# Attention feeding a mixture of experts: w1's first load in eight pieces, one transfer each for a unit's q and k, and a changed first microsecond

## The chip, the cores and the metric

The kernel runs on one core of a Trainium2 chip. The metric is the device time in microseconds of one execution. A core has five engines with a program each: TensorE (PE in the profile, its weight loads PEld), VectorE (DVE), ScalarE (ACT), GpSimd (POOL) and SyncE (SP). SyncE computes nothing: it issues DMA transfers, which 16 DMA engines carry out.

## The reference

First comes attention in chunks of 64 rows, for 8 batches, 8 heads, 576 rows and a head size of 64; then the heads of a row are put side by side (512 values), and each row goes through one expert of eight. Which expert is a matter of the rows before it: where the local gate is at least 0.5, the row keeps the expert of the row before.

```python
scores = scale * np.matmul(q_c, k_c.transpose(0, 1, 2, 4, 3))    # per chunk of 64 rows
attn = np.exp(scores - max);  attn = attn / (sum + 1e-09)
x = np.matmul(attn, v_c)                                          # heads side by side: [8, 576, 512]
e = argmax(x[b, s] @ w_gate) if s == 0 or local_gate[b, s] < 0.5 else prev_e
out[b, s] = p[e] * (np.maximum(x[b, s] @ w1[e], 0) @ w2[e])       # w1[e]: 512 x 1024, w2[e]: 1024 x 512
```

All arrays are f32. q, k and v are 9.4 MB each; one expert's w1 is 2 MB, and so is its w2.

## The kernel before, in words

The attention is cut into 18 units of 256 rows with all 8 heads (`place`, L134). Units 6 and 15 are made of four leftovers of 64 rows (`mixed_rows`, L141). A unit's q and k are loaded by `load_qk` (L144): two transfers of 256 KB for q and two for k. The first holds heads 0 to 3, the second heads 4 to 7; a partition takes 8 rows of one head, 2 KB, from each. All these loads are issued by SyncE, except unit 0's k, which ScalarE issues (L154). The mixed units take eight transfers of 128 KB (L149). v comes in two or four transfers of 256-byte rows (`load_v`, L159).

Then, per unit: copies put two heads side by side (`pair_heads`, L172, done by GpSimd but for unit 0; its copies carry line L190 or, on ScalarE, L188), TensorE transposes q and k (`qk_transposes`, L209, by `trans4`, L198), multiplies them into scores (`scores`, L226, matmuls at L233), VectorE takes the row maximum and subtracts it (L244, L247), ScalarE takes the exponential (L252), TensorE transposes the result (`p_transposes`, L264) and multiplies it with v (`values`, L273, L282), VectorE normalises and writes the rows of x (L294 to L296), and these are transposed, multiplied with the gate weights (`router`, L318) and stored to the scratch tensor `x_d` by SyncE (L346).

TensorE, ScalarE, VectorE and GpSimd run in an order written out by hand (`PAR`, L50): "start" for the first microseconds, "steady" for the periods i = 1 to 15, "drain" for the end of attention and the first expert tiles. A period works on several units at once: it loads q and k of unit i+5 and v of unit i+2, pairs heads of unit i+3, transposes q and k of unit i+2, takes the scores of unit i+1 and the values of unit i-1, and stores x of unit i-2. SyncE's queue follows the order in which the program issues: in a period q and k, then v, then x's store, then, in some periods, a piece of w1.

Expert 0's w1 is loaded within the attention stage (`load_w1`, L101) in four transfers of 128 rows of 4 KB, 512 KB each, at the ends of periods 4, 6, 8 and 10 (L880 and L881). In periods 8 to 15 `split` (L107) turns half a piece per period into a high part (ScalarE) and a low part (GpSimd).

PSUM, where TensorE writes, has three buffers for transposes (`ps_tr`, L120), used in turn. In "start" the order for TensorE is q's transposes of unit 0 (tokens t0a, t0b), k's (t0c, t0d), four of unit 1, then unit 0's scores (s0).

After attention the expert stage runs tiles of 128 gathered rows through w1 and w2 of their expert; the change does not touch it.

## Time and profile before

| what | us |
|---|---|
| median of 3 runs | 638.35 (638.34 to 639.34) |
| the profiled execution, whole | 638.56 |
| its span, first to last instruction | 636.8 |
| TensorE busy in the span | 608.1 (96%) |
| VectorE, ScalarE, GpSimd busy | 380.3, 255.8, 147.0 |

The profile is of one execution, and the span is what all its views divide up; 1.76 us of the execution lie around it. Busy time of TensorE is pipelined and its ends are modelled, so a busy TensorE is not one at its peak. In a row of the order of time, the first number is the start, the second the length, "x8" the instructions merged in the row, and the brackets give how long the engine was idle before it and what ended that. "issue" there means that nothing which the profile shows ended the wait.

### The profile page before, as it was taken

What the parts mean: (1) busy time and instruction counts of PE and PEld (TensorE: products, weight loads), DVE (VectorE), ACT (ScalarE), POOL (GpSimd) and SP (SyncE); (2) the same over time, 40 slices, a digit from 0 to 9 for tenths busy, and PEclk for the clock granted to TensorE, in tenths of its full rate; (3) what the DMA queues carried; (4) which work ended last, traced back from release to release, by engine and by line L of the source; (5) the groups of instructions that cost most, each with busy time, mean ns of one, the idle gap of its engine ahead of it and who ended that gap; (6) DMA issues with size and microseconds to landing.
All of it is one profiled execution on the core that took longest, in us unless ns stands there. A gap on an engine that the chain in (4) does not pass through costs nothing. (4 is left out here: it accounts for less than half of the span.)

```text
span 636.8 us, 17170 instructions
## 1 busy us (share of the span) xinstructions
PE 608.1 (96%) x5904; PEld 513.6 (81%) x5904; DVE 380.3 (60%) x990; ACT 255.8 (40%) x468; POOL 147.0 (23%) x219
## 2 busy tenths in 40 slices
PE   4899989889999999999999999999999999999995
PEld 4788777777779788789998996789888998788884
DVE  2677678887795667575434556763478533387231
ACT  4677667664421252532112443421465211343120
POOL 3353244550050302021021021031021221010201
PEclk9999999999999999999999999999999999999999
DMA  8999999998440245155021264452086511054111
GB/s 267 264 265 301 284 272 264 303 286 271 158 150 21 71 151 185 44 178 180 20 70 55 61 206 134 151 178 64 27 271 203 190 52 59 30 184 147 65 30 36
DMA packets 78355, 97.83 MB, mean 154 GB/s; under 512 B 42672, under 2 KB 46768, under 8 KB 78192
## 3 DMA queue, kind: packets, MB, share of 16 engines
q1 hardware_dynamic: 71744, 75.30, 37.9%
q0 software_dynamic: 6160, 19.99, 9.6%
q8 instruction: 84, 1.38, 0.9%
q14 instruction: 79, 0.65, 0.3%
q10 hardware_dynamic: 288, 0.52, 0.3%
HBM read 76.62 MB, written 19.69 MB: 151 GB/s over the span
## 5 line engine op out<-in xcount | busy, mean ns | idle before, releaser
L804 POOL DMA_INDIRECT out<-ysb,sidx x38 | 40.2, 1058 | 356.3 <-DVEq L1028 160.6
L743 PE MATMUL y<-w2h,hq 128*128 128x512 f32 x368 | 119.8, 395 | 1.3 <-DVE ysb L1078 1.0
L743 PEld LDWEIGHTS y<-w2h,hq 128*128 128x128 f32 x368 | 69.1, 188 | 16.9 <-issue 2.5
L743 PE MATMUL y<-w2l,hq 128*128 128x512 f32 x184 | 71.9, 391 | 0.0
L1050 PE MATMUL tr<-xp,w1h 128*128 128x256 f32 x528 | 67.0, 283 | 0.0
L1050 PEld LDWEIGHTS tr<-xp,w1h 128*128 128x128 f32 x528 | 65.5, 192 | 1.2 <-ACT w2h L1011 0.4
L743 PE MATMUL y<-w2h,hp 128*128 128x512 f32 x192 | 63.3, 397 | 0.3 <-ACT hp L690 0.3
L722 PE MATMUL h<-w1h,xp 128*128 128x512 f32 x208 | 60.5, 396 | 0.0
L1058 ACT ACTIVATE hq<-tr 128x256 fp32r<-128x256 f32 x51 | 18.9, 383 | 68.4 <-PE tr L1050 44.8
L1078 DVE TENSOR_SCALAR ysb<-y,ppr 128x512 f32<-128x512 f32 x33 | 24.8, 751 | 34.4 <-PE y L743 30.3
L722 PEld LDWEIGHTS h<-w1h,xp 128*128 128x128 f32 x208 | 38.1, 188 | 7.4
L694 POOL DMA_INDIRECT xg<-x_d,gidx x36 | 38.5, 1069 | 19.8 <-issue 14.5
L743 PEld LDWEIGHTS y<-w2h,hp 128*128 128x128 f32 x192 | 36.0, 188 | 8.1 <-ACT hp L690 0.5
L789 ACT ACTIVATE hsb<-h 128x512 f32<-128x512 f32 x26 | 14.1, 596 | 66.1 <-PE h L722 49.1
L1059 DVE SCALAR_TENSOR_TENSOR hq<-tr,hq 128x256 fp32r<-128x256 f32 x51 | 21.1, 423 | 32.3 <-ACT hq L1058 28.6
L743 PEld LDWEIGHTS y<-w2l,hq 128*128 128x128 f32 x184 | 34.6, 188 | 6.9 <-DVEq L1028 0.3
L743 PE MATMUL y<-w2l,hp 128*128 128x512 f32 x96 | 37.5, 390 | 0.0
L1018 DVE TENSOR_TENSOR w1l<-raw,w1h 128x1024 fp32r<-128x1024 f32 x28 | 32.4, 1221 | 8.3 <-ACT w1h L1011 4.9
L691 DVE TENSOR_TENSOR xp<-tr,xp 128x512 fp32r<-128x512 f32 x39 | 25.5, 686 | 18.6 <-ACT xp L690 15.8
L1050 PE MATMUL tr<-xp,w1l 128*128 128x256 f32 x264 | 35.3, 283 | 0.0
L1018 DVE TENSOR_TENSOR w2l<-raw,w2h 128x1024 fp32r<-128x1024 f32 x28 | 32.8, 1223 | 1.2 <-issue 1.2
L1050 PEld LDWEIGHTS tr<-xp,w1l 128*128 128x128 f32 x264 | 33.3, 192 | 0.0
(242 smaller groups left out, 1152.7 us busy)
## 6 DMA issues: line engine op xcount, KB each, us to landing
raw<-in_moe_w SPq DMA_DIRECT2D x72, 512.0 KB
x_d<-xs SPq DMA_DIRECT2D x16, 528.0 KB
v<-in_v SPq DMA_DIRECT2D x20, 256.0 KB
qt<-in_q SPq DMA_DIRECT2D x16, 256.0 KB
lenth<-in_q SPq DMA_DIRECT2D x16, 256.0 KB
lentl<-in_k SPq DMA_DIRECT2D x16, 256.0 KB
kt<-in_k SPq DMA_DIRECT2D x14, 256.0 KB
raw<-in_v SPq DMA_DIRECT2D x6, 256.0 KB
```

Of the source, the lines that this page charges most:

```text
L691: lambda: V.tensor_tensor(lo, box["ps"], hi.bitcast(F32), ALU.subtract)]
L694: nc.gpsimd.indirect_dma_start(out=dst, out_offset=None, in_=src, in_offset=bass.IndirectOffsetOnAxis(ap=gidx[t].bitcast(U32), axis=0))
L722: nc.tensor.matmul(hs[:, j], xs[a][:, c], W1[w][c][:, 512 * j:512 * j + 512], start=(c == 0 and n == 0), stop=(c == 3 and n == 2))
L743: nc.tensor.matmul(y, h_of(t, f // 4)[a][:, f % 4], W2[w][c][:, f % 2, :], start=(f == 0 and n == 0), stop=(f == 7 and n == 2))
L789: nc.scalar.activation(hsb[:, 512 * j:512 * j + 512], hs[:, j], AF.Relu)
L804: nc.gpsimd.indirect_dma_start(out=out, out_offset=bass.IndirectOffsetOnAxis(ap=sidx[t].bitcast(U32), axis=0), in_=ysb, in_offset=None, bo ...
L1018: V.tensor_tensor(lo[c], raw[c], hi[c].bitcast(F32), ALU.subtract)
L1050: nc.tensor.matmul(hb[:, 256 * n:256 * n + 256], W1[w][c][:, P * (f + n):P * (f + n) + P], XP[:, x, c].rearrange("p s t -> p (s t)"), star ...
L1058: nc.scalar.activation(hi, ps, AF.Relu)
L1059: V.scalar_tensor_tensor(lo, ps, 0.0, hi.bitcast(F32), ALU.max, ALU.subtract)
L1078: V.tensor_scalar(ysb, y, pr, None, ALU.mult)
```

## The change

Three things change. Expert 0's w1 comes in eight transfers of 256 KB (128 rows of 2 KB), one at the end of each of the periods 4 to 11. For the units 1 to 15 that are not mixed, q is one transfer of 512 KB and so is k; the heads in the two column halves are then 0, 2, 4, 6 and 1, 3, 5, 7 instead of 0 to 3 and 4 to 7, and `values` reads v and writes x accordingly. For unit 0 the first halves of q and k go by SyncE's queue and the second halves by ScalarE's, and TensorE gets five matmuls of the identity with itself, 256 columns each, as its first work; their result is not read.

```diff
+    def heads_by_two(i):
+        return 0 < i < NS - 2 and not mixed_rows(i)
+
     def load_qk(i):
...
+                if heads_by_two(i):
+                    nc.sync.dma_start(
+                        dst.rearrange("p (j n) -> p j n", j=2),
+                        src[b, :, s0:s0 + n, :].rearrange("h (p r) d -> p h (r d)", r=8))
+                    continue
                 for j in range(2):
-                    (nc.scalar if i == 0 and src is k else nc.sync).dma_start(
+                    (nc.scalar if i == 0 and j == 1 else nc.sync).dma_start(
                         dst[:, 8 * D * j:8 * D * j + 8 * D],
                         src[b, 4 * j:4 * j + 4, s0:s0 + n, :].rearrange("g (p r) d -> p g (r d)", r=8))
...
-    def values(pT, vt, xs, fine=False):
+    def values(pT, vt, xs, fine=False, by_two=False):
         box = {}
+        if by_two:
+            xv = xs[:, :, 0:C].rearrange("p c (h j d) -> p j c h d", j=2, d=D)
+        else:
+            xv = xs[:, :, 0:C].rearrange("p c (j h d) -> p j c h d", j=2, d=D)
...
-                        vt[cp][64 * cc:64 * cc + 64, 4 * j + h, 0:D + 1],
+                        vt[cp][64 * cc:64 * cc + 64, 2 * h + j if by_two else 4 * j + h, 0:D + 1],
...
-                    xs[:, :, 256 * j:256 * j + 256].rearrange("p c (h d) -> p c h d", d=D),
+                    xv[:, j],
...
-        return values(pTs.pop(i), vts.pop(i), xss[i], fine)
+        return values(pTs.pop(i), vts.pop(i), xss[i], fine, heads_by_two(i))
...
         nc.scalar.activation(warm, ident[:, 0:1], AF.Exp)
+        awake = ps_tr.tile([P, 4, P], F32, name="tr")
+        for _ in range(5):
+            nc.tensor.matmul(awake[:, 0:2], ident, ident.unsqueeze(1).to_broadcast([P, 2, P]), start=True, stop=True)
...
-        if i in (4, 6, 8, 10):
-            load_w1(0, i // 2 - 2)
+        if 4 <= i < 12:
+            c, col = divmod(i - 4, 2)
+            col = slice(512 * col, 512 * col + 512)
+            nc.sync.dma_start(raw1[c][:, col], w1[0, P * c:P * c + P, col])
```

## Rows read from the trace of the kernel before

**Rows 1.** The page, its first part: busy time and instructions of each engine.

```profile
PE 608.1 (96%) x5904; PEld 513.6 (81%) x5904; DVE 380.3 (60%) x990; ACT 255.8 (40%) x468; POOL 147.0 (23%) x219
```

**Rows 2.** Busy time by stretch: PE, PEld, DVE, ACT, POOL, clock, DMA share, GB/s.

```profile
0.00:24.00 24.00, 14.23 (x306) 12.74 (x310) 8.88 (x16) 12.01 (x21) 8.80 (x30) 1.00 0.91 271
24.00:140.00 116.00, 106.51 (x2531) 88.46 (x2523) 90.30 (x256) 81.47 (x142) 55.62 (x109) 1.00 0.96 277
140.00:636.80 496.80, 487.40 (x3082) 412.43 (x3082) 281.13 (x720) 162.30 (x307) 82.56 (x80) 1.00 0.36 119
```

**Rows 3.** TensorE's waits between 24 and 140 us: total, times, longest.

```profile
PE sc L233 <- issue: 3.4, 5, 1.4
PE o L282 <- issue: 2.0, 2, 1.3
...
PE lg L324 <- issue: 0.7, 1, 0.7
```

**Rows 4.** The start in order of time, all engines, 0 to 16 us.

```profile
1.43 0.28 POOL masks.py:199 TENSOR_SCALAR_AFFINE_SELECT ident<-ident 128x128 f32<-128x128 f32 x1
...
5.59 0.61 POOL L190 COPY kr<-kt 128x512 f32<-128x512 f32 x1 [3.87 <-DMA kt<-in_k]
...
6.18 0.62 ACT L188 COPY qr<-qt 128x512 f32<-128x512 f32 x1 [2.62 <-DMA qt<-in_q]
...
6.95 1.94 PE L198 MATMUL tr<-ident,qr 128*128 128x128 f32 x8 [6.95 <-ACT qr L188]
...
8.68 1.92 PE L198 MATMUL tr<-ident,kr 128*128 128x128 f32 x8
...
11.37 1.16 PE L233 MATMUL sc<-kT,qT 64*64 64x64 f32 x64
...
12.95 1.09 PE L198 MATMUL tr<-ident,kr 128*128 128x128 f32 x8
```

**Rows 5.** Busy time by stretch, the first transfers (columns as in rows 2).

```profile
2.00:4.10 2.10, 0.00 (x0) 0.00 (x0) 0.00 (x0) 1.49 (x2) 0.00 (x0) 1.00 0.83 251
4.10:5.40 1.30, 0.00 (x0) 0.00 (x0) 0.00 (x0) 0.00 (x0) 0.00 (x0) 1.00 1.05 405
```

**Rows 6.** The order of time, GpSimd and TensorE, units 2 and 3.

```profile
15.01 1.17 POOL L190 COPY kr<-kt 128x512 f32<-128x512 f32 x2 [0.60 <-DMA kt<-in_k]
...
18.36 1.06 PE L198 MATMUL tr<-ident,kr 128*128 128x128 f32 x8
18.96 1.17 POOL L190 COPY qr<-lenth 128x512 f32<-128x512 f32 x2 [2.78 <-DMA lenth<-in_q]
...
22.31 1.09 PE L198 MATMUL tr<-ident,qr 128*128 128x128 f32 x8
```

**Rows 7.** The order of time, SyncE: loads of w1.

```profile
57.10 0.46 SPq L102 DMA_DIRECT2D raw<-in_moe_w  x1
...
73.66 0.46 SPq L102 DMA_DIRECT2D raw<-in_moe_w  x1
...
108.17 0.46 SPq L102 DMA_DIRECT2D raw<-in_moe_w  x1
```

**Rows 8.** The order of time, TensorE, around three stops.

```profile
64.89 0.58 PE L233 MATMUL sc<-kT,qT 64*64 64x64 f32 x24 [1.44 <-issue]
...
80.81 0.50 PE L282 MATMUL o<-v,pT 64*64 64x65 f32 x18 [1.30 <-issue]
...
116.44 0.64 PE L324 MATMUL lg<-xT,wg 128*32 128x256 f32 x8 [0.68 <-issue]
```

**Rows 9.** The DMA view of 57 to 62 us, then of 62.5 to 63.5.

```profile
DMA packets 1229, 1.54 MB, mean 308 GB/s; under 512 B 690, under 2 KB 690, under 8 KB 1229
...
q8 instruction: 1, 0.02, 5.5%
```

**Rows 10.** Lines L154 and L190: ns least/median/most, first and last start us.

```profile
L154 SPq DMA_DIRECT2D lenth<-in_q x16: 540/621/2696, 12.1 to 117.7; - x16
...
L190 POOL COPY qr<-lenth x18: 609/614/679, 19.0 to 129.0; 128x512 f32<-128x512 f32 x18
```

## The prediction

> **What bounds the kernel now.** I read the page first: TensorE is busy for 96% of the span [rows 1]. Then I cut the span into three stages [rows 2]. In the first 24 us TensorE is idle for 9.8 us. From 24 to 140 us, in the attention periods, it is idle for 9.5 us, while the DMA engines' share is 0.96. From 140 us on it is idle for 9.4 of 496.8 us, and the DMA share is 0.36. So TensorE's work sets the time, and a microsecond of its idle time before 140 us that goes away should come off the total, as long as nothing that it needs then comes late. The other engines are well below it in every stage.

> Next I asked what it waits for between 24 and 140 us [rows 3]. Three entries, 3.4, 2.0 and 0.7 us in eight stops, are put down to "issue": no semaphore and no transfer ends them. Last I read the start in order of time [rows 4] and how far the first transfers lead their use [rows 6].

> **The start, q first.** Today q goes by SyncE's queue and k by ScalarE's. k's copies start at 5.59, q's at 6.18, and TensorE's first transposes, which want q, at 6.95 [rows 4]. The change sends half of q by each queue, then half of k by each. By 4.1 us the queues had moved 527 KB, and by 5.4 us as much again, together the 1.05 MB of unit 0's q and k [rows 5]. The whole was in use 0.8 us after that (5.4 to 6.18). With the same lag q alone, 524 KB, is there at 4.1 + 0.8 = 4.9 us; the latest I allow is 5.59, when a pair was first in use today. One copy of 0.62 and the 0.15 us between copy and transpose (6.80 to 6.95) let q's transposes start at 5.7 (at the latest 6.4). k then comes where q came, 6.18, and is copied by 6.8.

> **The start, TensorE warm.** The granted-clock column of the windows reads 1.00 from the start [rows 2], and can't tell the first microseconds apart. The durations can: eight transposes take 1.94 us at 6.95 and 1.92 at 8.68, but 1.09 at 12.95 [rows 4]. [...] I take the rise at the scores, 4.4 us after its first instruction. The five new matmuls need only the identity, complete at 1.71 [rows 4]. A plain f32 matmul is two instructions here (a unit's 32 score matmuls are 64 in the row at 11.37), and 128 columns take 0.21 us apart at the low clock (1.94 us less a tail of 0.24, over eight). So 256 columns are 0.43 us, and five matmuls 5 x 2 x 0.43 = 4.3 us: from 1.8 to 6.1. That holds q's transposes up by 0.4 us against 5.7, and the clock rises at 1.8 + 4.4 = 6.2, just as they start.

> Then the 16 transposes take 2 x 1.09 instead of 3.65 (6.95 to 10.60) and end at 8.3; with the 0.77 us from there to the scores today (10.60 to 11.37) the scores start at 9.05 instead of 11.37: 2.3 us. k's copies (6.8) are done before its transposes want them (7.2). If the clock rises only after this stretch, the 4.42 us from 6.95 to 11.37 stay and start at 6.1: 0.85 us. All the bounds above put q's transposes ahead of 6.95, so a loss is excluded.

> How much of it lasts? After the scores the chain runs through VectorE and ScalarE and moves as a whole; the transfers don't move. k of unit 2 and q of unit 3 are taken the moment they land (GpSimd's copies at 15.01 and 18.96 end a wait for the DMA) and are copied by 16.18 and 20.13; TensorE uses them at 18.36 and 22.31 [rows 6]. That is a lead of 2.18 us for each, so at most 2.2 us can go through. **I take 2.2 us, bounds 0.85 and 2.2.**

> **w1 in halves.** Four loads of 512 KB, three of them at 57.10, 73.66 and 108.17 [rows 7], become eight of 256 KB, one in each of periods 4 to 11, behind x's store as before. TensorE has stops of 1.44, 1.30 and 0.68 us that end at 64.89, 80.81 and 116.44, each 7 to 8 us after such a load, all ended by "issue" [rows 8]. A packet of instructions (queue q8) moves between 62.5 and 63.5, as the first of these stops begins (64.89 - 1.44 = 63.45) [rows 9]. I read them as TensorE out of code: the packet stood behind data. At the 308 GB/s of 57 to 62 us [rows 9], 512 KB are 1.70 us ahead of it and half is 0.85. Halving takes 0.85 + 0.85 + 0.68 = 2.38 us off these stops. Against it, four periods without w1 get 0.85 us more in the way: nothing where code was in time with room to spare, all of it where it was just in time, 4 x 0.85 = 3.4 at most. The other five stops of [rows 3], 2.7 us in all, tell how near the rest is to being late; I take a bit under half of the 3.4, 1.5. **Net gain 0.9 us, bounds a gain of 2.4 and a loss of 1.0.** The splits still use a piece four periods after its load, and the same 2 MB move. The four more issues on SyncE, 0.46 us each in these rows [rows 7], stand in front of loads with the lead shown next.

> [...]

> **One transfer for a unit's q, one for its k.** For 13 units (1 to 5 and 7 to 14) four issues of about 0.6 us on SyncE [rows 10] become two of 512 KB, so SyncE is spared between nothing and 13 x 2 x 0.6 = 16 us over some 100. TensorE gets nothing of that: no load ends one of its waits after 24 us, and the last q transfer is issued at 117.7 and last copied at 129.0 [rows 10], a lead of 11 us against the 5.4 us in which the first four transfers came. That lead also covers TensorE running 3 us earlier. Bytes, 2-KB rows and the order of the units are the same; the new order of heads changes strides alone, so the value matmuls and VectorE's normalising write keep their shapes and counts. I take 0. What it touches is code: a transfer of 512 KB may be one longer block in front of an instruction packet. Upper bound: each of the eight stops grows by 0.85 us, 6.8. Lower bound: SyncE's evener feeding clears the stops that w1 leaves, a gain of 6.1 - 2.4 = 3.7.

> **Sum.** 2.2 + 0.9 + 0 = 3.1 us. The profiled execution took 638.56 us (span 636.8 and 1.76 around it), so 635.5 there; the median of the runs is 638.35, 0.2 lower, so I say 635.3. After 140 us nothing is edited, and I carry the gain through.

> **Rivals.**
> A. Only the start moves. [...] For it: the fourth w1 load has no large stop behind it. The time is 638.35 - 2.2 = 636.15. [...]
> B. Long transfers starve TensorE of code. [...] Price: half of the eight stops grow by 0.85, 3.4 us, and the w1 pieces cost their 1.0; with the start's gain 638.35 - 2.2 + 4.4 = 640.55, slower. It decides once the stops grow by over 3.5 us in sum, from 6.1 to more than 9.6. For it: a DMA share near 1. Against: the bytes ahead of a packet don't change when two transfers that follow each other become one.
> [...]

> **Chances.** Forecast 0.45, A 0.19, C 0.21, B 0.15. About 0.2%, 1.3 us, is what a measurement of this kernel can tell from no change: below 637.1 is faster, above 639.6 slower. Forecast and A are faster but for the ends of their bounds, 0.62; C with the mild part of the others is 0.24; the hard part of B 0.14. Range: from 633.6 (w1 at its best 2.4 and a little of the other stops) to 639.3 (start at 0.85, some 1.8 us of new stops). Left out are B and a little at the bottom. Forecast and A alone lie in 633.6 to 637.1.

> **What would show it.** Right: ten new matmul instructions from 1.8 to about 6.1; q's eight transposes near 6.1 in about 1.1 us; unit 0's scores near 9; GpSimd waiting longer for k of unit 2 and q of unit 3, TensorE no more idle than now; its "issue" waits between 24 and 140 us near 5 us, none above 1 us behind w1; 26 fewer q and k issues; from 140 us all as now, 3 us earlier. Wrong: transposes of 1.9 us after the new matmuls (C); TensorE waiting for a load after 24 us; "issue" waits above 9 us (B); or the gain there at 140 us and gone by 600.

## The result, and the profile after

The changed kernel is **slower**: 646.30 us median of 20 runs (638.54 to 650.91) against 639.22 of 20 runs of the kernel before (637.45 to 641.41), ratio 1.0079, 95% interval 1.0060 to 1.0099. Ratios, here and below, are of the fast runs alone, here 16 of the 20, while the medians and ranges are of all runs, so these two medians divide to more, 1.0111. I had said 635.3, range 633.6 to 639.3. The profiled execution took 641.01 us (span 639.2), one of the quickest of the 20: its mean granted clock is 0.997, while 17 of the 20 show 0.996 or less. So its rows understate the loss, and the runs that follow must find the rest.

First the page and the same three stretches as [rows 1, 2] (columns as there):

```profile
PE 611.4 (96%) x5914; PEld 515.5 (81%) x5914; DVE 380.0 (59%) x990; ACT 256.1 (40%) x468; POOL 147.3 (23%) x219
...
0.00:24.00 24.00, 18.89 (x340) 16.21 (x341) 10.26 (x19) 12.57 (x22) 8.84 (x30) 1.00 0.94 279
24.00:140.00 116.00, 104.16 (x2479) 86.01 (x2479) 87.23 (x251) 80.88 (x140) 55.17 (x109) 1.00 0.95 274
140.00:639.20 499.20, 488.36 (x3107) 413.31 (x3104) 282.55 (x721) 162.61 (x307) 83.34 (x81) 1.00 0.36 119
```

TensorE's busy time from 24 to 140 us fell by 2.4 us (106.51 to 104.16): it did less there although its scores began 1.4 us earlier. The order of time at the start (TensorE, as in [rows 4]):

```profile
1.78 4.63 PE L611 MATMUL tr<-ident 128*128 128x256 f32 x10 [1.78 <-POOL ident masks.py:199]
6.21 1.81 PE L206 MATMUL tr<-ident,qr 128*128 128x128 f32 x8
7.85 1.04 PE L206 MATMUL tr<-ident,kr 128*128 128x128 f32 x8
...
9.98 1.16 PE L241 MATMUL sc<-kT,qT 64*64 64x64 f32 x64
```

The scores start at 9.98 instead of 11.37. q's eight transposes still take 1.81 us and only k's take 1.04, so TensorE sped up near 7.8 us here, after the new matmuls and most of q's transposes. The trace's record of the granted clock begins there, at 7.77 us, with 1.00; in the kernel before it begins at 11.30. Then TensorE's waits between 24 and 140 us (as [rows 3]) and its stops over 1 us in that part of the order of time:

```profile
PE sc L241 <- issue: 2.4, 4, 1.2
...
PE o L294 <- issue: 1.7, 3, 1.1
PE lg L345 <- issue: 1.5, 1, 1.5
PE o L294 <- DVE pr L255: 1.1, 1, 1.1
PE tr L206 <- ACT kT L196: 1.1, 1, 1.1
```

```profile
30.01 0.57 PE L294 MATMUL o<-v,pT 64*64 64x65 f32 x21 [1.05 <-issue]
...
42.46 0.63 PE L241 MATMUL sc<-kT,qT 64*64 64x64 f32 x27 [1.18 <-issue]
...
49.50 0.33 PE L345 MATMUL lg<-ident,lT 128*128 128x128 f32 x1 [1.52 <-issue]
...
71.80 0.63 PE L206 MATMUL tr<-ident,kr 128*128 128x128 f32 x4 [1.12 <-ACT kT L196]
78.25 0.69 PE L294 MATMUL o<-raw,pT 64*64 64x65 f32 x32 [1.12 <-DVE pr L255]
```

No stop ends near 64.9, 80.8 or 116.4 any more, but others have come elsewhere: "issue" is 5.6 us in eight stops, against 6.1. The stops at 71.80 and 78.25 are put down to ScalarE and VectorE, yet stand in the same places as the others. Counted in TensorE's instructions (6,425 that load weights or steer plus 5,904 matmuls in the kernel before), seven stops of over 0.15 us here, these two among them, and five in the kernel before come at instruction 193 and a multiple of 256, or within two of it, that is at the start of a block of 256 instructions; and each of these twelve ends 2.3 to 2.6 us after a packet of code (queue q8, 16 KB each) starts to move. I read them as TensorE waiting for its next block of code. These boundaries hold 6.6 us of stops here and 4.9 in the kernel before. The other three "issue" stops of the kernel before, 1.3 us that end from 137.0 to 138.5, lie at no boundary.

### The profile page after: what moved, and what is told of

Read it like the earlier page. It is cut to its first block, busy times and chain, and to the rows that moved or that the text cites. A ratio compares the mean times of both kernels' runs of the same rounds, so it can differ in the third digit from the quotient of the medians.

```text
span 639.2 us, 17142 instructions
## 1 busy us (share of the span) xinstructions
PE 611.4 (96%) x5914; PEld 515.5 (81%) x5914; DVE 380.0 (59%) x990; ACT 256.1 (40%) x468; POOL 147.3 (23%) x219
```

## The experiments

Ratios are to runs of the kernel before on the same chip. "issue" and "load" are TensorE's waits from 24 to 140 us ended by nothing that the profile shows and by a DMA; "end" is the time from the start of TensorE's last matmul to the end of the span. The last two come from one execution each, and scatter between executions: "issue" by up to some 5 us among kernels of the same time, as e5 will show.

| kernel | median us | ratio (95%) | issue, load us | end us |
|---|---|---|---|---|
| before | | 1 | 6.1, 0 | 6.28 |
| after | 646.30 | 1.0079 (1.0060 to 1.0099) | 5.6, 0 | 7.84 |
| e1 single q and k transfers alone | 648.46 | 1.0159 (1.0134 to 1.0184) | 10.6, 0 | 6.52 |
| e2 all but the single transfers | 639.11 | 1.0036 (1.0021 to 1.0051) | 4.4, 0 | 7.08 |
| e3 w1 in pieces alone | 639.30 | 1.0032 (1.0012 to 1.0052) | 2.0, 2.7 | 6.21 |
| e4 start alone | 638.05 | 1.0018 (0.9997 to 1.0038) | 3.3, 0.4 | 7.22 |
| e5 order of heads alone | 638.07 | 0.9997 (0.9973 to 1.0022) | 1.2, 0 | 6.06 |
| e6 448 + 64 KB | 657.28 | 1.0295 (1.0260 to 1.0330) | 3.2, 7.3 | 6.06 |
| e7 start, v first | 646.91 | 1.0142 (1.0107 to 1.0178) | 1.1, 0 | 7.28 |
| e8 v first alone | 646.16 | 1.0124 (1.0085 to 1.0164) | 1.7, 0 | 6.44 |
| e9 single transfers, paced | 642.78 | 1.0058 (1.0030 to 1.0086) | 5.3, 0 | 6.20 |
| e10 half of k by ScalarE | 649.79 | 1.0162 (1.0108 to 1.0215) | 5.3, 0 | 6.40 |
| e11 before, no w1 bytes | 636.80 | 0.9970 (0.9943 to 0.9997) | 3.8, 0 | 6.30 |
| e12 start, no w1 bytes | 637.47 | 0.9989 (0.9956 to 1.0023) | 2.9, 0 | 7.13 |
| e13 q first alone | 639.05 | 0.9994 (0.9970 to 1.0018) | 2.1, 0.5 | 6.00 |
| e14 warm alone | 640.77 | 1.0013 (0.9990 to 1.0035) | 2.7, 0.6 | 7.94 |
| e15 start, 12 instructions | 640.50 | 1.0015 (0.9992 to 1.0038) | 3.6, 0.5 | 6.94 |
| e16 start, 40 instructions | 642.36 | 1.0040 (1.0012 to 1.0067) | 3.7, 0 | 7.10 |

**Each part by itself.** e1 is the kernel before with only `heads_by_two`, its single transfers and the new order of heads; e2 the changed kernel without these; e3 the kernel before with only the last hunk of the diff, e4 with only the first microseconds' two hunks.

> The kernel before with the single 512-KB transfers for q and k alone (13 units, heads by two); w1 in four loads and the start as before. Theory 1 (code waits behind whole 512-KB transfers): this part is the loss; the median is 5 to 9 us above before (644 to 648), the runs scatter by several us, TensorE's waits ended by 'issue' between 24 and 140 us sum to 8 us or more against 6.1. Theory 2 (the start: the clock rises early and falls again in the sparse first periods): same as before, within 1 us. Theory 3 (w1's pieces): same as before.

> The changed kernel with q and k again in two transfers of 256 KB each; w1 in eight pieces, warm TensorE and q first stay. Theory 1: the loss is gone; 1 to 3 us below before (636 to 638). Theory 2: still 4 us or more above before, mean granted clock in the runs about 0.993. Theory 3: still 4 us or more above before, clock near 0.999.

> The kernel before with w1 in eight 256-KB pieces alone. Theory 1: within 1.5 us of before; the three stops of 1.44, 1.30 and 0.68 us behind w1 become smaller, others may come. Theory 2: the same. Theory 3: 4 us or more above before.

> The kernel before with the changed start alone (five matmuls of the identity, q by both queues ahead of k). Theory 1: 1 to 2 us below before, scores of unit 0 at 10.0 instead of 11.4. Theory 2: 4 us or more above before in most runs, mean clock 0.99, the clock falling again before 40 us. Theory 3: as theory 1.

The single transfers cost 1.6% alone. Without them e2 still loses 0.4%, where I had expected it 1 to 3 us below before, and e4 does not show its 1 to 2 us either. The parts do not add up: the changed kernel has the single transfers and the rest and loses 0.79%, half of what the single transfers lose alone and 0.43% more than e2 (each against its own chip's runs). No run has the single transfers with w1's pieces or with the start alone, so what takes the other half back is open. The same view of waits in e1:

```profile
PE o L294 <- issue: 7.7, 5, 2.0
PE sc L241 <- issue: 2.9, 2, 2.3
```

10.6 us of "issue" instead of 6.1, in seven stops, all at block boundaries, each ending 2.2 to 2.5 us after a packet of code starts. How one such stop comes about: TensorE's order of time, SyncE's, and the DMA view of 88.1 to 94.7 and of 94.7 to 95.6 us, all of e1:

```profile
88.12 0.50 PE L294 MATMUL o<-v,pT 64*64 64x65 f32 x18 [1.69 <-issue]
...
93.91 0.79 PE L241 MATMUL sc<-kT,qT 64*64 64x64 f32 x34
96.98 0.63 PE L241 MATMUL sc<-kT,qT 64*64 64x64 f32 x28 [2.28 <-issue]
...
87.08 0.62 SPq L102 DMA_DIRECT2D raw<-in_moe_w  x1
87.79 0.95 SPq L157 DMA_DIRECT2D qt<-in_q  x1
88.85 0.63 SPq L157 DMA_DIRECT2D kt<-in_k  x1
89.57 2.37 SPq L173 DMA_DIRECT2D raw<-in_v  x2
...
DMA packets 1098, 1.94 MB, mean 294 GB/s; under 512 B 314, under 2 KB 314, under 8 KB 1098
...
q1 hardware_dynamic: 1098, 1.94, 93.5%
...
q8 instruction: 1, 0.02, 6.4%
```

A block of 256 instructions begins at 88.12, and from there to 94.7 the queue of data alone moves: 1.94 MB. Between 87.08 and 88.85 SyncE had issued w1, q and k, 512 KB each. Only then comes a packet of code. TensorE had nothing to do from 94.70 (96.98 - 2.28). Over the blocks that begin between 24 and 140 us, from a block's first instruction to the next packet of code, the mean is 2.95 us in e1, over 3 us in 11 of 19, against 2.60 us and 5 of 18 in the kernel before, where two more blocks see no packet before the next begins; the trace does not tell which engine's code a packet holds. 1,098 packets of data, some 69 for each of the 16 engines, went ahead of the packet of code here, if the code was asked for when the block began, which the trace does not show.

What a long stop costs besides itself, in the windows of e1 (PE, PEld, DVE, ACT, POOL, clock, DMA share, GB/s):

```profile
55.90:56.76 0.86, 0.86 (x25) 0.48 (x24) 0.00 (x0) 0.00 (x0) 0.00 (x0) 1.00 0.95 326
56.76:60.17 3.41, 3.41 (x20) 3.27 (x17) 2.19 (x6) 1.25 (x2) 1.17 (x2) 0.50 0.93 296
...
97.00:97.72 0.72, 0.72 (x49) 0.72 (x52) 0.00 (x0) 0.00 (x0) 0.48 (x1) 1.00 1.05 385
97.72:101.13 3.41, 3.41 (x42) 3.29 (x31) 2.62 (x6) 1.17 (x2) 0.00 (x0) 0.50 0.89 242
```

The stops of 2.02 us (to 55.90) and 2.28 us (to 96.98) are each followed, 0.7 to 0.9 us later, by 3.41 us at a granted clock of 0.50; after none of e1's shorter ones does it fall. This does not hold for all kernels: in e7 a stop of 2.49 us leaves the clock at 1.00, and in e13 it falls at 137.15 us with no stop over 0.9 us ahead of it from 24 us on. At 0.50, 3.41 us lose 1.7 us of work, an estimate, so e1's 10.2 us over the execution of before are 4.5 of stops, 3.4 of clock and 2.3 that I can't place, 0.7 of them lost before its 400th matmul (28.02 instead of 27.31). That bears on the changed kernel's median too: its runs' mean clock is 0.994, against 0.997 in its profile, and 0.003 of 640 us is 1.9 us. That is a rough estimate, since the mean takes in the low clock behind the last matmul (0.50 from 635.8 us on in the profile), which costs nothing.

The start as e2 has it (TensorE):

```profile
1.78 4.35 PE L611 MATMUL tr<-ident 128*128 128x256 f32 x10 [1.78 <-POOL ident masks.py:199]
5.96 1.04 PE L206 MATMUL tr<-ident,qr 128*128 128x128 f32 x8
...
8.97 1.16 PE L241 MATMUL sc<-kT,qT 64*64 64x64 f32 x64
```

In e3 and e4 "issue" is less (2.0 and 3.3 us), but TensorE now waits for v. The waits of e3 (24 to 140 us):

```profile
PE o L282 <- DMA lenth<-in_v: 1.3, 1, 1.3
PE o L282 <- issue: 1.1, 1, 1.1
...
PE sc L233 <- issue: 0.9, 2, 0.5
...
PE o L282 <- DMA v<-in_v: 0.6, 2, 0.4
```

These rows don't account for e3's loss of 2 us: "issue" fell by 4.1 us and the waits for loads are 2.7, and e3's profiled execution, 643.95 us, is the second slowest of its 12. What costs e3 its 2 us stays open.

**Why single transfers cost: length, order of heads, or pace.** e5 keeps the new order of heads but loads it in halves; e6 cuts each single transfer into 448 and 64 KB; e9 adds a tiny one behind each.

```diff
+                    for j in range(2):                                    # e5
+                        nc.sync.dma_start(dst[:, 8 * D * j:8 * D * j + 8 * D],
+                            src[b, j::2, s0:s0 + n, :].rearrange("g (p r) d -> p g (r d)", r=8))
...
+                    for p0, p1 in ((0, 28), (28, 32)):                    # e6
+                        nc.sync.dma_start(
+                            dst[4 * p0:4 * p1].rearrange("p (j n) -> p j n", j=2),
+                            src[b, :, s0 + 8 * p0:s0 + 8 * p1, :].rearrange("h (p r) d -> p h (r d)", r=8))
...
+                    nc.sync.dma_start(pace[2 * (i % 2) + (src is k)],     # e9
+                                      src[b, 0, s0:s0 + 16, 0:8])
```

> The kernel before with only the new order of heads (0, 2, 4, 6 in the first half of q's and k's tiles, 1, 3, 5, 7 in the second), each half still its own 256-KB transfer. Theory (the length of a transfer costs, not the order of heads): same as before, ratio 1.000 within 0.002, stops at the ends of code blocks 4 to 6 us in sum (before 4.94), none over 2 us. Rival O (the order costs: VectorE writes and TensorE reads with other strides): the 1.6% of the kernel with single transfers stays, 648 us, with o and xs instructions longer than before's.

> The kernel with single q and k transfers, but each cut again into 448 KB and 64 KB, so that SyncE issues four transfers a unit as before. Theory L (a long block of data in front of an instruction packet): 7/8 of the length stays, so most of the loss stays: ratio 1.010 to 1.016, stops at block ends 8 us or more in sum, some over 2 us. Rival P (SyncE, spared two issues a unit, feeds the queue sooner and so keeps more bytes ahead of a packet): with four issues again the loss goes, ratio 1.000 to 1.004, stops 4 to 6 us.

> The kernel with single 512-KB q and k transfers, and behind each of them a transfer of 16 rows of 32 bytes to a spare tile, so that SyncE issues four a unit as before while the long transfers stay whole (448 + 64 KB did not show this: the 64 KB lay on 16 partitions and slowed the queue to 224 GB/s). Theory L (a long transfer in front of an instruction packet): the loss stays, ratio 1.012 to 1.018, stops at block ends 8 us or more in sum. Rival P (SyncE's spared issues keep more bytes queued): the loss goes, ratio 1.000 to 1.005, stops 4 to 6 us.

The order of heads costs nothing: 0.9997, and VectorE's 30 writes of x from 24 to 140 us take 691 ns on the mean in e5 as in the kernel before. I had expected 4 to 6 us of stops at block ends in e5; it has 1.2 us of "issue" where the kernel before has 6.1, though both take the same time. So that sum, from one execution, tells little between 1.2 and 6.1; e1's 10.6 lies outside. e6 answers another question: it misses both theories, with 3.2 us of "issue" but 7.3 of load and a clock of 0.91 from 60 to 140 us, and the queue itself is slower, 224 GB/s from 24 to 60 us. The two parts lie on 112 and on 16 partitions; why the rate fell is not shown, since no row here shows the engines one by one. e9 tells most. The windows of e1, e9 and the kernel before from 24 to 60 us, in that order (columns as above):

```profile
24.00:60.00 36.00, 31.91 (x727) 27.17 (x726) 25.50 (x60) 23.08 (x40) 15.60 (x53) 0.95 1.01 294
```

```profile
24.00:60.00 36.00, 33.51 (x739) 28.16 (x731) 24.68 (x59) 22.49 (x39) 14.66 (x51) 0.91 0.94 268
```

```profile
24.00:60.00 36.00, 35.12 (x872) 29.79 (x866) 27.13 (x65) 26.19 (x46) 16.32 (x54) 1.00 0.95 268
```

With two issues a unit instead of four, the DMA engines' mean share is 1.01 and they move 294 GB/s; with the two tiny transfers, 0.62 us of SyncE each, they are back at 0.94 and 268, as before (0.91 and 272 up to 34.10 us, ahead of a fall of the clock). The transfers are as long as in e1, but of the 1.59% loss 0.58 is left, between the two ranges that I had given. So some two thirds of the loss go when two tiny transfers are put in; the two ratios come from different chips, and the profiled execution of e9 still has one stop of 2.2 us, around whose end the clock falls for 6.8 us (0.91 in its row). Why they go is argued, not shown. My reading is SyncE's pace: spared 1.2 us a unit, it puts the next transfers into the queue sooner, and a packet of code finds fewer gaps. That the tiny transfers themselves make the gaps is not excluded, and a full queue alone did not stop TensorE in e5. From 60 to 100 us e5 has the fullest queue of the three, with 306 GB/s, and 0.2 us of "issue", where e1 has 6.8 us, and e9, at 282 GB/s, 1.9 (e5, then e1):

```profile
60.00:100.00 40.00, 39.39 (x948) 32.86 (x941) 31.44 (x84) 30.96 (x55) 17.21 (x26) 1.00 1.01 306
60.00:100.00 40.00, 33.17 (x789) 28.01 (x788) 23.42 (x57) 24.39 (x42) 12.07 (x19) 0.97 0.98 285
```

e10 was to show pace without length, by giving the second half of k to ScalarE's queue.

```diff
-                    (nc.scalar if i == 0 and src is k else nc.sync).dma_start(
+                    (nc.scalar if src is k and (i == 0 or (j == 1 and i < NS - 2)) else nc.sync).dma_start(
```

> The kernel before with the second 256-KB half of each unit's k issued by ScalarE's queue instead of SyncE's: no transfer is longer, SyncE is spared one issue a unit (half of what single transfers spare). Theory L: no loss from code, ratio 0.998 to 1.003, stops at block ends 4 to 6 us. Rival P: half of the loss or more, ratio 1.006 or above, stops above 7 us.

It doesn't tell: ScalarE now issues k of later units ahead of its copies for unit 0, so these, and all behind them, start some 6 us later (ScalarE in e10):

```profile
9.83 2.33 ACTq L154 DMA_DIRECT2D lentl<-in_k  x3
12.20 0.62 ACT L188 COPY qr<-qt 128x512 f32<-128x512 f32 x1 [7.32 <-DMA v<-in_v]
```

**Where the start's gain goes: the loads.** e7 and e8 issue v ahead of q and k in the steady periods, on e4 and on the kernel before. e11 and e12 are the kernel before and e4 without w1's 2 MB in the attention.

```diff
-    "steady": "lq lv s*8 ...
+    "steady": "lv lq s*8 ...                                              # e7, e8
...
-            split(w1h[c][:, col], w1l[c][:, col], raw1[c][:, col], nc.gpsimd)
+            nc.gpsimd.memset(w1h[c][:, col].bitcast(F32), 0.0)            # e11, e12, without load_w1(0, ...)
+            nc.gpsimd.memset(w1l[c][:, col].bitcast(F32), 0.0)
```

> The start's part alone (TensorE warm, q ahead of k in the first unit), and in each steady period v's two loads issued ahead of q's and k's four on SyncE. Theory V (the start's 2.2 us were given back because TensorE, running earlier, waits for v loads near 91 and 101 us): those waits go, the gain stays to the end, ratio 0.996 to 0.998 (some 636 against 638). Rival S (the gain is lost to stops at block ends that fall elsewhere, not to v): ratio 1.000 to 1.002 with no wait for v left and 2 us more of stops.

> The kernel before with only the order on SyncE changed, v ahead of q and k in each steady period. Both theories: nothing to gain where no load was waited for, ratio 1.000 within 0.002, stops 4 to 6 us. If this alone is faster by 0.2% or more, a gain of the run with the start's part is not the start's.

> The kernel before without its four loads of w1 for expert 0 in the attention (2 MB, some 7 us of the transfers at 290 GB/s); w1's high and low parts are filled with zeros by GpSimd instead, so the products of expert 0 are left out in value but not in instructions. If the transfers are a bound beside TensorE: faster by more than the stops behind w1 alone, 2 to 5 us, ratio 0.992 to 0.997. If only the stops behind w1 cost: 2.4 us at most, ratio 0.996 to 1.000.

> The start's part (TensorE warm, q ahead of k) on top of the kernel without w1's 2 MB. Theory D (the transfers, busy for 0.95 of the attention, take back what TensorE gains at the start): with 7 us of transfers gone the start's gain shows at the end, 1.5 to 2.2 us below the other kernel without w1's bytes. Rival N (the gain is lost elsewhere, in the fall of the block ends or in the tail): no difference between the two, within 0.6 us.

Putting v first is a miss of both theories: 1.2 to 1.4% slower, with "issue" down to 1.1 and 1.7 us. A group of VectorE's instructions in e8 (busy us, mean ns, idle time before and what ended it) shows the new wait, which the kernel before does not have:

```profile
L296 DVE TENSOR_TENSOR xs<-o,rs 128x512 f32<-128x512 f32 x29 | 20.1, 691 | 13.4 <-DMA x_d<-xs 12.6
```

VectorE waits 12.6 us for a free buffer of x, that is for x's store. The store stands behind v, q and k on SyncE's queue in both kernels, but the queue's own waits in e8 have grown in front of q and k, from 2.0 us in four waits for GpSimd in the kernel before to 15.2 in these eight:

```profile
SPq L154 <- POOL kr L190: 7.2, 3, 2.8
SPq L154 <- POOL w1l L109: 5.9, 4, 2.5
SPq L154 <- POOL qr L190: 2.1, 1, 2.1
```

Which of these waits came first the runs don't separate. The order on SyncE's queue weighed more than w1's pieces (0.3%), if less than the single transfers (1.6%). Without w1's bytes the kernel is 0.3% faster (e11), but the start gives nothing there either: 637.47 against 636.80. That speaks against the transfers as what takes the gain back, and for rival N of that run. It is no proof: the two ratios differ by 0.19%, with about 0.4% of uncertainty either way, which just reaches the 1.5 us that the other theory asked for.

**Where the start's gain goes: the end.** In the five kernels so far with the ten matmul instructions "end" is 7.1 to 7.8 us, in the others 6.1 to 6.5. e13 has q first alone, e14 the matmuls alone; e15 and e16 warm for the same time with 12 and with 40 instructions instead of 20.

```diff
-        for _ in range(5):
-            nc.tensor.matmul(awake[:, 0:2], ident, ident.unsqueeze(1).to_broadcast([P, 2, P]), start=True, stop=True)
+        for m in (4, 4, 2):                                               # e15
+            nc.tensor.matmul(awake[:, 0:m], ident, ident.unsqueeze(1).to_broadcast([P, m, P]), start=True, stop=True)
...
+        for _ in range(10):                                               # e16
+            nc.tensor.matmul(awake[:, 0], ident, ident, start=True, stop=True)
```

> Only q's halves ahead of k's in the first unit, no new matmuls. Theory T (the twenty new TensorE instructions move every block end, and with it an instruction packet into the last scatters): from the last matmul to the end 6.1 to 6.5 us as before; first scores 0.5 to 1.2 us earlier than 11.4 to 12, and that stays: ratio 0.998 to 0.9995. Rival Q (the other order of the first transfers is what lengthens the end): 7.1 us or more there, ratio 0.999 to 1.002.

> Only the ten new matmul instructions with their ten weight loads, k still ahead of q. Theory T: the stretch after the last matmul 7.1 to 7.3 us; transposes at full clock, first scores about 9.8 to 10.5; ratio 0.999 to 1.002. Rival Q: 6.1 to 6.5 us there, and a gain of 1 us or more that stays, ratio 0.997 to 0.999.

> The start's part with three wide matmuls (512, 512 and 256 columns) in place of five of 256: the same time, but 12 TensorE instructions in place of 20, so that block ends move by 12. First scores 9 to 9.5 as with five. Theory T: the stretch after the last matmul changes with the count, to something between 6.1 and 7.3 us. If it stays at 7.1 to 7.3 whatever the count, it hangs on something else of the start's part.

> The start's part with ten matmuls of 128 columns in place of five of 256: the same time, but 40 TensorE instructions in place of 20. Theory T: the stretch after the last matmul differs from 7.1 to 7.3 us in this kernel or the one with 12; where it is back at 6.1 to 6.5 and the attention's stops are no more than 5 us, the start's gain shows in the median, ratio 0.996 to 0.998. If it stays at 7.1 to 7.3 for 12, 20 and 40 alike, the shift of the blocks is not the cause.

e14 misses at the start. Its ten matmul instructions run from 1.78 to 6.42 us as in the changed kernel, then TensorE waits 0.60 us for q, and the transposes are as slow as before (TensorE):

```profile
7.02 1.97 PE L198 MATMUL tr<-ident,qr 128*128 128x128 f32 x8 [0.60 <-ACT qr L188]
8.78 1.92 PE L198 MATMUL tr<-ident,kr 128*128 128x128 f32 x8
```

The scores start at 11.41, where I had expected 9.8 to 10.5. So the new matmuls do not speed up q's transposes in every execution: q's eight transposes take 1.04 us in e2, e4, e7 and e16, 1.54 in e15, 1.63 in e12, 1.81 in the changed kernel and 1.97 in e14.

The matmuls go with a longer end, and the order of q and k does not: 6.00 in e13, 7.94 in e14. GpSimd's last two scatters in e13, and in e14:

```profile
625.15 0.98 POOL L804 DMA_INDIRECT out<-ysb,sidx  x1 [11.88 <-DMA out<-ysb,sidx]
630.48 0.97 POOL L804 DMA_INDIRECT out<-ysb,sidx  x1 [4.34 <-POOLq L1193]
```

```profile
628.79 0.98 POOL L807 DMA_INDIRECT out<-ysb,sidx  x1 [11.88 <-DMA out<-ysb,sidx]
635.14 0.97 POOL L807 DMA_INDIRECT out<-ysb,sidx  x1 [5.37 <-POOLq L1196]
```

5.33 us lie between them without the matmuls, 6.35 with them. The DMA view of the stretch from 8 us before TensorE's last matmul to 1.2 us after it (621.0 to 630.2 in e13, 624.6 to 633.8 in e14) has one packet of code in the first and two in the second:

```profile
q8 instruction: 1, 0.02, 1.1%
```

```profile
q8 instruction: 2, 0.03, 2.8%
```

All eight kernels with these matmuls have two packets of code 2.2 to 2.9 us ahead of the last matmul, the ten others have one, at 2.5 (e10: 1.6); the last-but-one scatter is written from 2.3 us ahead on, and the last scatter waits for its end. 12, 20 and 40 instructions do the same (6.94, 7.22, 7.10), so the theory that the count decides falls as I had put it. What the eight share is one packet of code more in the whole execution, 85 (q8) instead of the 84 of each of the ten others; that this packet is the cause was only seen beside the delay and not tried by itself. The eight also take one buffer of `ps_tr` more, which shifts the turn of its three; no run separates the two. The end takes 0.7 to 1.7 us, and the scores come at most 2.4 us earlier (e2); where the rest goes in the median is open. e4's profiled execution, one of the quickest of its 12, still has its last matmul 2.7 us earlier than the kernel before (627.77 against 630.50). With q first alone the scores come at 9.72, 1.6 us earlier, and its ratio, 0.9994, allows a gain of 0.3% and none. These times of the start scatter too: in the eight kernels whose start is not edited the scores start anywhere from 11.37, in the kernel before, to 13.31, in e6. No kernel that does all the work is shown to beat the kernel before.

## Why the prediction was wrong

- **One transfer for a unit's q, one for its k: "I take 0".** This step failed. Alone it costs 1.59%, 10 us, beyond my upper bound of 6.8; in the changed kernel it is 0.43 of the 0.79%, some 2.8 us. I wrote that SyncE is spared up to 16 us and that TensorE gets nothing of it. It got 10.6 us of stops at block boundaries in e1, which I read as waits for code, instead of 4.9. My bound counted half a megabyte more per stop and nothing for the granted clock, which in e1 fell to 0.50 twice (3.4 us lost). The argument against rival B, that the bytes ahead of a packet don't change, looked at two transfers and not at how soon the next ones follow; that this is the reason is my reading of e9 and not shown. B's direction was right; its price, 4.4 us, and its chance, 0.15, were too low.
- **w1 in halves: "Net gain 0.9 us".** This step failed as well: e3 is 0.32% slower, 2 us, and the bound of 1.0 us of loss was too small. The stops that I put down to w1 are gone in e3 (2.0 us of "issue" instead of 6.1), but e5, with w1 whole, has only 1.2, so that w1's pieces took them away is not shown. Nor were all eight code: the three of 1.3 us near 138 lie at no boundary. The step weighed code alone, though v stands in the same queue, and in e3 TensorE waits for v, 2.7 us; whether that is its loss stays open.
- **The start: "I take 2.2 us".** Where q's transposes ran fast, the start came as I said: in e2 they take 1.04 us, and the scores start at 8.97, where I said 9.05. In the changed kernel k's copies start at 6.07 and 6.14, much as I said, but q's transposes take 1.81 us, and the scores start at 9.98: 1.4 us, not 2.3. In e14 all 16 transposes stay slow, 1.97 and 1.92 us for eight. The 4.4 us from TensorE's first instruction to the rise came from a single execution, and no run shows that they hold in others: the record of the granted clock begins 4.35 us after that instruction in the kernel before, but 5.99 us after it in the changed kernel, and in e14 the transposes are slow until 10.70 us, 8.9 us after it. What failed besides is "moves as a whole" and the gain carried through after 140 us: the end is 0.7 to 1.7 us longer with the new matmuls, and e4 shows no gain (1.0018). The 2.18 us of lead of unit 2's k, which I took for the cap, did not bind: e2's matmul at the place of the 401st (the ten new ones not counted) starts at 24.94, still 2.4 us ahead (27.35).
- **The sum.** w1 and the start were to gain 3.1 us; e2, which has these two, loses 0.36%, 2.3 us. So 5.4 us of the error lie there and some 2.8 in the single transfers, though alone these cost most.
- **"That lead also covers TensorE running 3 us earlier"** holds for q and k and was never worked out for v, whose transfers TensorE waits for in e3, e4 and e13 to e15.
- **What would show it wrong.** I named "issue" above 9 us as B's sign. e1 has 10.6; the profiled execution of the changed kernel only 5.6, partly because two stops at block ends are put down to other engines, partly because it is one of the quickest.

## What to carry to other kernels

In this kernel, where the DMA engines are busy for 0.96 of the attention stage and packets of code move among those of data, issuing fewer, larger transfers was not free: alone it cost 1.59%, TensorE stood still for 10.6 us instead of 4.9 at block boundaries, and in e1 two stops of over 2 us were each followed by 3.41 us at a granted clock of 0.50. Cost a DMA edit by every stream that shares the DMA engines, code and the load with the shortest lead first, and cost the issue order as carefully as the bytes. A gain at the start is only a gain when the end is seen to keep it: measure it on the parts, since one profiled execution can lie among the quickest, and the stops in it can differ by 5 us between kernels of the same time.
